# A delta-rule attention with two MoE layers on one core: the second layer's weights converted six tiles later

## The chip, the cores and the metric

The kernel runs on one core of one Trainium2 chip. The metric is the device time of one execution in microseconds (us); three runs of the kernel before gave 930.33, 930.95 and 936.27, and their median is 930.95 us. Lower is better.

## What is computed

A recurrent attention over 768 steps (4 batches, 8 heads of width 48) writes 3072 tokens of width 384. Two dense layers follow on each token: the first goes 384 to 1024 with a softmax-weighted activation and a layer norm and back to 384, the second goes 384 to 2048, takes the square of the ReLU, and goes back to 384. Cut to what matters:

```
for t in range(S):                       # attention, k_n = k / |k|
    y[t] = q[t] @ state
    state = state + b[t] * outer(k_n[t], v[t] - k_n[t] @ state)
h = x @ w_in;  s = h * softmax(h)        # first layer
x1 = layer_norm(s) * g_ln @ w_out
r = relu(x1 @ w2_in)                     # second layer
out = (r * r) @ w2_out
```

The weights arrive as 64-bit floats and are needed as 32-bit floats.

## The kernel before, in words

**Tiles.** The tokens are taken as 24 tiles of 128 (`NT`). For every tile TensorE forms the Gram products of keys and queries (`e_tile`, up to ten tiles ahead), a small triangular matrix is inverted for groups of 2 to 4 tiles (`inversion`), the blocks of the inverse are loaded back from DRAM in two shapes and joined (`prep`), a product with them is formed for each half of the tile (`zstep`), and two recurrent steps follow (`chain`). The groups start at tiles 0, 4, 7, 11, 15, 19 and 22 (`G0`). The first group is inverted on VectorE, the other six on GpSimd, by hundreds of small multiply and add instructions (lines 900 and 917) that end in line 942. ScalarE then makes the transposed copy (line 959), and both forms go to DRAM (`tscr`, `uscr`), from where `prep` loads them (`tbd`, `t`).

**First layer.** It runs beside the attention, two to four tiles behind it: `moe1_front` (transposes on line 1207, products into `p_h` on line 1218, softmax and norm sums on ScalarE and VectorE), `moe1_back` (transposes on line 1320, the high and low parts `zh` and `zl` from `split`, line 433) and `moe1_out` (products into `p_x` on line 1340, for two tiles at once). Each float product is done as three products of rounded parts, hence `hi` and `lo` in `split`.

**Second layer.** It starts when the attention is over, since its weights take the SBUF space of the attention pool (`open_m2`). From about 545 us to the end TensorE runs only its products (lines 1483 and 1527).

**Weights.** `load_w` turns a chunk of 64-bit numbers into 32-bit ones: a DMA into one of two `raw` buffers, one ScalarE instruction (line 466) into one of two `wst` buffers, and four VectorE instructions (lines 474, 485, 500, 510). The chunks of the second layer, 12 of `w2_in` and 16 of `w2_out`, are then written back to DRAM as 32-bit numbers (`load_w2`, `w2s` and `wos`), because there is no room for them in SBUF yet; `fill_w2` reads them again when the pool of the second layer is open.

**What sets the order.** Every instruction group is handed to `Plan.add` with its engine, an estimated cost, what it reads and writes, a priority, and further operations that it must come after (`after`). `Plan.order` then simulates the engines with these costs, forwards and backwards in 12 rounds: the first round goes by the priorities given, each later one by how late an operation may be as the round before found it, and the best round's order is emitted. The order on every engine, on SyncE's DMA queue too, is thus fixed before the kernel runs; an instruction that is late holds up all that stand behind it on its engine. A priority counts in the first round only; an operation in `after` counts in all.

The change touches the loop over tiles (line 1616), where the second layer's chunks are handed to the planner, and the first VectorE instruction of `load_w` (line 474).

Of the kernel before, what the change touches and what calls it, by code (L numbers as in the profile page):

```python
# [114 lines left out]
class Plan:  # L115
# [19 lines left out]
    def add(self, eng, cost, fn, r=(), w=(), prio=0.0, size=0, after=()):  # L135

        i = len(self.ops)
        deps = set(after)
        for k in r:
            if k in self.writer:  # L140
                deps.add(self.writer[k])
            if k in self.BANKS:

                deps.update(j for j in self.readers.get(k, ()) if self.ops[j][0] != eng)
            self.readers.setdefault(k, []).append(i)
        for k in w:
            if k in self.writer:
                deps.add(self.writer[k])
            deps.update(self.readers.get(k, ()))
            self.writer[k], self.readers[k] = i, []  # L150
        deps.discard(i)
        self.ops.append((eng, cost, fn, prio, deps, size))
        return i
# [108 lines left out]
def c_dve(n, fast=False):  # L262
    return 0.07 + n / (1920.0 if fast else 960.0)


def c_act(n, sbuf=False):
    return (0.095 if sbuf else 0.053) + n / 1200.0
# [8 lines left out]
def tile_delta_moe_moe(  # L276
# [16 lines left out]
    plan = Plan()  # L293
# [4 lines left out]
    def dma(dst, src, r=(), w=(), prio=0.0, size=0):  # L298

        return add("sp", 0.06, lambda: nc.sync.dma_start(dst(), src()), r, w, prio, size, gate)  # L300
# [40 lines left out]
    def const(i, n, u=False):  # L341
        return (cst_u if u else cst)[:, i : i + 1].to_broadcast([P, n])
# [96 lines left out]
        )  # L439


    n_w, first_inv = [0], []

    def load_w(src, n, prio):

        i = n_w[0] % 2
        n_w[0] += 1
        w = wst_[i][:, 0:n]
        kw, kr = ("A", "wst", i), ("A", "raw", i)
        if src.dtype == F32:  # L450
            dma(lambda: w, lambda: src, (), [kw], prio - 1, P * n * 4)
            return w, kw
        raw, wu = raw_[i][:, 0:n], w.bitcast(U32)
        up, low = raw[:, :, 1], raw[:, :, 0]
        dma(
            lambda: raw.rearrange("p n t -> p (n t)"),
            lambda: src.bitcast(U32),
            (),
            [kr],
            prio - 1,  # L460
            P * n * 8,
        )
        add(
            "act",
            c_act(n, True),
            lambda: act.activation(out=w, in_=up.bitcast(F32), func=AF.Abs),
            [kr],
            [kw],
            prio,
        )  # L470
        add(
            "dve",
            c_dve(n),
            lambda: v.scalar_tensor_tensor(
                out=w, in0=w, scalar=F64_LO, in1=const(3, n), op0=ALU.max, op1=ALU.min
            ),
            [],
            [kw],
            prio,
            after=first_inv,  # L480
        )
        add(
            "dve",
            c_dve(n),
            lambda: v.scalar_tensor_tensor(
                out=wu,
                in0=wu,
                scalar=3,
                in1=const(5, n, True),
                op0=ALU.logical_shift_left,  # L490
                op1=ALU.bitwise_and,
            ),
            [],
            [kw],
            prio,
        )
        add(
            "dve",
            c_dve(n),
            lambda: v.scalar_tensor_tensor(  # L500
                out=wu, in0=up, scalar=0xC0000000, in1=wu, op0=ALU.bitwise_and, op1=ALU.bitwise_or
            ),
            [kr],
            [kw],
            prio,
        )
        add(
            "dve",
            c_dve(n),
            lambda: v.scalar_tensor_tensor(  # L510
                out=wu,
                in0=low,
                scalar=29,
                in1=wu,
                op0=ALU.logical_shift_right,
                op1=ALU.bitwise_or,
            ),
            [kr],
            [kw],
            prio,  # L520
        )
        return w, kw
# [40 lines left out]
    def load_w2(i, prio):  # L563

        if i < 12:
            c, s = i // 4, slice((i % 4) * 512, (i % 4) * 512 + 512)
            w, kw = load_w(w2i[c, :, s], 512, prio)
            dma(lambda: w2s[c][:, s], lambda: w, [kw], [("w2s", c, i % 4)], prio, P * 2048)
        else:
            f = i - 12  # L570
            w, kw = load_w(w2o[f], DM, prio)
            dma(lambda: wos[f], lambda: w, [kw], [("wos", f)], prio, P * DM * 4)
# [193 lines left out]
    def gammas(g, prio):  # L766

        n = 2 * (G0[g + 1] - G0[g])
        w = n * NP
        be, gm = be_[g % 2], gm_[g % 2]  # L770
        x, y, u = nrm_[g % 3].rearrange("p s q -> p (s q)")[:, 0:w], ny[:, 0:w], ntt[:, 0:w]
        b = be[:, 0:w]
        kn = [("A", "nrm", g % 3, s) for s in range(n)]
        kbe, ky, kgm = ("A", "be", g % 2), ("A", "ny"), ("A", "gm", g % 2)
        if n < GS:
            add("pool", 0.1, lambda: pool.memset(be[:, w:], 0.0), (), [kbe], prio - 1)
        dma(
            lambda: b,
            lambda: betat[:, 2 * G0[g] * NP : 2 * G0[g + 1] * NP],
            (),  # L780
            [kbe],
            prio - 1,
            P * 128,
        )

        def dv(fn, r, w):
            add("dve", c_dve(HB), fn, r, w, prio)

        dv(
            lambda: v.tensor_tensor(out=x, in0=x, in1=const(0, w), op=ALU.max), (), kn  # L790
        )
        rsqrt(y, x, u, HB, kn, [ky], prio)
        dv(lambda: v.tensor_tensor(out=x, in0=x, in1=y, op=ALU.mult), [ky], kn)
        dv(
            lambda: v.tensor_tensor(out=x, in0=x, in1=const(2, w), op=ALU.add), (), kn
        )
        dv(lambda: v.reciprocal(y, x), kn, [ky])
        dv(lambda: v.tensor_tensor(out=b, in0=b, in1=y, op=ALU.mult), [ky], [kbe])
        dv(lambda: v.tensor_tensor(out=b, in0=b, in1=y, op=ALU.mult), [ky], [kbe])

        gt = p_z[:, NP * 112 : NP * 112 + HB]

        def mm():
            for hb in range(4):
                sl = slice(hb * HB, hb * HB + HB)
                pe.matmul(gt[sl], be[sl], ident[sl, sl], start=True, stop=True)

        add("pe", 0.22, mm, [kbe], [("A", "z")], prio)
        add("act", c_act(HB), lambda: act.copy(gm, gt), [("A", "z")], [kgm], prio)
# [779 lines left out]
    for t in range(NT + 3):  # L1589
        if t < NT:  # L1590
            for g in range(2, NG):
                if t == max(1, G0[g] - 5):
                    gammas(g, t + PR["inv"])
                    inversion(g, "pool", t + PR["inv"])
            tp = t + PR["first"] if t < T1 else t
            chain(2 * t, tp + PR["chain"])
            zstep(2 * t + 1, tp + PR["z"])
            chain(2 * t + 1, tp + PR["half"] + PR["chain"])
            if t + 1 < NT:
                tp = t + PR["first"] if t + 1 < T1 else t  # L1600
                prep(t + 1, tp + PR["prep"])
                zstep(2 * t + 2, tp + PR["z1"] + PR["z"])
            if t + LA < NT:
                e_tile(t + LA, t + PR["e"])
                norms(t + LA, t + PR["norms"])
        if t == NT - 1:
            add("x", 0.0, open_m2, (), [*plan.keys("A"), ("m2",)], t)
        if 2 <= t < NT + 2:
            moe1_front(t - 2, t + PR["mf"])
            if t == NT + 1:  # L1610
                add("x", 0.0, open_mb, [("m2",)], [*plan.keys("W"), ("mb",)], t)
        if t >= 3:
            moe1_back(t - 3, t + PR["mb"])
            if (t - 3) % 2:
                moe1_out((t - 3) // 2, t + PR["mo"])
        for i in (2 * t - 4, 2 * t - 3):
            if 0 <= i < 28:
                load_w2(i, t + PR["w2"])
    add("x", 0.0, open_ps, [("m2",)], [("h", 0), ("h", 1), ("tr",), ("x1",), ("ps",)], NT + 3)
    for n in range(4):  # L1620
# [75 lines left out]
```

## Time and profile before

| | us |
|---|---|
| median of the three runs | 930.95 |
| the profiled execution | 934.67 |
| its span, first to last instruction | 932.7 |
| TensorE busy (matmul) | 864.9 |
| VectorE busy | 519.5 |
| ScalarE busy | 487.3 |
| GpSimd busy | 365.2 |

The profile shows one execution on the chip. PE is TensorE's matmuls, PEld its weight loads, DVE is VectorE, ACT is ScalarE, POOL is GpSimd, and SP or SPq is SyncE, which issues all DMAs. PEclk is the share of full speed that TensorE's clock was granted: 1.00 is 2.4 GHz and 0.50 is 1.2 GHz. "A <- B" in a table of waits means that A stood idle until B was done. L433 is line 433 of the kernel.

### The profile page before, as it was taken

How to read it: one execution, taken by the hardware profiler on the slowest of the kernel's cores; microseconds unless marked ns; L12 is line 12 of the kernel's file. 1: busy time of each engine (PE TensorE's matmuls, PEld its weight loads, DVE VectorE, ACT ScalarE, POOL GpSimd, SP SyncE). 2: the span in 40 equal slices, each digit the busy share in tenths (PEclk: the TensorE clock that was granted, in tenths of full speed). 3: DMA queues.
4: the chain of work that ended last, by engine and by line, in shares of the span. 5: the costliest groups of instructions: out<-in, count | busy, mean ns of one | idle time of the engine just before them, and what ended most of it. 6: DMA issues, size and time to landing. Idle time of an engine off the chain costs nothing.

```text
span 932.7 us, 23189 instructions
## 1 busy us (share of the span) xinstructions
PE 864.9 (93%) x9144; PEld 806.9 (87%) x9144; DVE 519.5 (56%) x1063; ACT 487.3 (52%) x1069; POOL 365.2 (39%) x898
## 2 busy tenths in 40 slices
PE   7349789989998999999998999999999999999998
PEld 6347678867887888888887999999999999999998
DVE  6996887786856896634435655343343434343332
ACT  5335787666756766666565644333333434343333
POOL 6399889899747947987500000000000000000000
PEclk8566898989998999999999999999999999999999
DMA  8827876858687577442314432001010101000000
GB/s 243 212 85 192 202 225 177 231 169 235 201 221 198 144 226 184 120 143 68 101 44 136 132 106 63 15 6 47 1 51 1 51 1 52 1 26 1 26 1 26
DMA packets 129244, 101.75 MB, mean 109 GB/s; under 512 B 84080, under 2 KB 106608, under 8 KB 129136
## 3 DMA queue, kind: packets, MB, share of 16 engines
q1 hardware_dynamic: 129136, 100.28, 38.4%
q8 instruction: 72, 1.18, 0.6%
q14 instruction: 36, 0.29, 0.1%
HBM read 70.88 MB, written 29.36 MB: 107 GB/s over the span
## 4 chain that ended last, share of the span: by engine, by line
PE 70%; DVE 8%; POOL 8%; DMA 7%; SPq 2%; ACT 2%; issue 2%; POOLq 0%; ACTq 0%; DVEq 0%
PE acc L1527 22%; PE h L1483 21%; PE p_x L1340 8%; PE p_h L1218 7%; PE p_z L1098 3%; POOL it L917 2%; POOL itmp L900 2%; SPq L300 2%; PE p_tr L1320 2%; PE p_a L1139 2%; DVE itmp L900 1%; DVE it L917 1%; DMA vt<-in_vtok_dram 1%; PE p_ep L684 1%; DMA m<-in_ktok_dram 1%
## 5 line engine op out<-in xcount | busy, mean ns | idle before, releaser
L1504 DVE TENSOR_TENSOR xt<-xt 128x384 f32<-128x384 f32 x128 | 71.5, 559 | 163.7 <-ACT xt L1496 163.5
L1496 ACT ACTIVATE xt<-h 128x384 f32<-128x384 f32 x128 | 62.9, 492 | 167.8 <-PE h L1483 167.7
L1483 PE MATMUL h<-x1h,w2h 128*128 128x384 f32 x384 | 128.9, 336 | 0.0
L1483 PE MATMUL h<-x1l,w2h 128*128 128x384 f32 x384 | 128.6, 335 | 0.0
L1483 PE MATMUL h<-x1h,w2l 128*128 128x384 f32 x384 | 128.3, 334 | 0.0
L917 POOL TENSOR_TENSOR it<-it,itmp 128x72 f32<-128x72 f32 (+37 forms) x255 | 110.1, 446 | 5.1
L900 POOL TENSOR_TENSOR itmp<-it 128x72 f32<-128x72 f32 (+37 forms) x255 | 109.3, 443 | 1.9
L1527 PE MATMUL acc<-woh,xl 128*128 128x384 f32 x258 | 87.4, 339 | 0.0
L1527 PE MATMUL acc<-wol,xh 128*128 128x384 f32 x258 | 87.3, 338 | 0.0
L1340 PE MATMUL p_x<-zh,wgh 128*128 128x256 f32 x288 | 85.7, 298 | 1.5 <-ACT xo L1354 1.5
L1527 PE MATMUL acc<-woh,xh 128*128 128x384 f32 x258 | 86.9, 337 | 0.0
L1340 PE MATMUL p_x<-zl,wgh 128*128 128x256 f32 x288 | 81.5, 283 | 1.0 <-DVE zl L433 1.0
L1340 PE MATMUL p_x<-zh,wgl 128*128 128x256 f32 x288 | 81.6, 283 | 0.0
L433 DVE TENSOR_TENSOR xl<-xt,xh 128x384 fp32r<-128x384 f32 x86 | 48.0, 558 | 45.7 <-ACT xh L428 45.5
L1483 PEld LDWEIGHTS h<-x1h,w2l 128*128 128x128 f32 x384 | 72.1, 188 | 0.0
L1483 PEld LDWEIGHTS h<-x1h,w2h 128*128 128x128 f32 x384 | 72.1, 188 | 0.0
L1483 PEld LDWEIGHTS h<-x1l,w2h 128*128 128x128 f32 x384 | 72.1, 188 | 0.0
L428 ACT CAST xh<-xt 128x384 fp32r<-128x384 f32 x86 | 44.1, 513 | 47.8 <-DVE xt L1504 46.7
L1218 PE MATMUL p_h<-w1h,xh 128*128 128x512 f32 x144 | 65.0, 451 | 0.1
L1098 PE MATMUL p_z<-m,tbd 128*128 128x112 f32 x384 | 59.9, 305 | 0.7 <-ACT tbd L1068 0.5
L1218 PE MATMUL p_h<-w1h,xl 128*128 128x512 f32 x144 | 59.1, 410 | 0.1
L1218 PE MATMUL p_h<-w1l,xh 128*128 128x512 f32 x144 | 58.8, 408 | 0.0
(197 smaller groups left out, 2152.0 us busy)
## 6 DMA issues: line engine op xcount, KB each, us to landing
kql<-in_kin_dram SPq DMA_DIRECT2D x24, 512.0 KB
kqe<-in_kine_dram SPq DMA_DIRECT2D x40, 192.0 KB
raw<-in_w2i_dram SPq DMA_DIRECT2D x12, 512.0 KB
raw<-in_w2o_dram SPq DMA_DIRECT2D x16, 384.0 KB
gscr<-g SPq DMA_DIRECT2D x21, 256.0 KB
m<-in_ktok_dram SPq DMA_DIRECT2D x24, 192.0 KB
vt<-in_vtok_dram SPq DMA_DIRECT2D x24, 192.0 KB
x1scr<-xo SPq DMA_DIRECT2D x12, 384.0 KB
```

The source lines that it names most:

```text
L300: return add("sp", 0.06, lambda: nc.sync.dma_start(dst(), src()), r, w, prio, size, gate)
L428: add("act", c_act(n), lambda: act.copy(hi(), src()), r, [w[0]], prio)
L433: lambda: le.tensor_tensor(out=lo(), in0=src(), in1=hi().bitcast(F32), op=ALU.subtract),
L900: lambda tm=tm, j=j, nr=nr, w_=w_, c0=c0, c1=c1: eng.tensor_tensor(out=tm, in0=it[:, j + 1 :, j : j + 1].to_broadcast([P, nr, w_]), in1=it ...
L917: lambda tm=tm, j=j, c0=c0, c1=c1: eng.tensor_tensor(out=it[:, j + 1 :, c0:c1], in0=it[:, j + 1 :, c0:c1], in1=tm, op=ALU.add,),
L1098: pe.matmul(zp[:, p].rearrange("q (j c) -> q j c", j=7), tb[:, i * NP + p], m[:, i, :, p], start=True, stop=True,)
L1218: pe.matmul(p_h[:, sl], xx[:, c], ww[:, c, sl], start=(c == 0 and k == 0), stop=(c == 2 and k == 2),)
L1340: pe.matmul(p_x1[:, 0 : 2 * P], ww[:, f, c * P : c * P + P], zz[:, f], start=(f == 0 and k == 0), stop=(f == 7 and k == 2),)
L1483: pe.matmul(late["h2", ih], late[ww][:, c, s], xx[:, c], start=(c == 0 and k == 0), stop=(c == 2 and k == 2),)
L1496: lambda: act.activation(out=rt, in_=late["h2", ih], func=AF.Relu),
L1504: lambda: v.tensor_tensor(out=gg, in0=rt, in1=rt, op=ALU.mult),
L1527: pe.matmul(late["acc", a], gg[:, a * P : a * P + P], late[ww][:, f], start=(f == 0 and k == 0), stop=(f == 15 and k == 2),)
```

## The change

The chunks of the second layer are handed out in the loop pass of tile 8 and the following ones, no longer from tile 2 on, and the first VectorE instruction of each chunk must come after the `zs` copy of the second half of that pass's tile. So the two chunks of pass t wait for `zstep(2t+1)`. The DMA of the raw chunk and the ScalarE instruction have no such condition. The instructions themselves are the same, 28 chunks with four VectorE instructions each.

```diff
-    n_w, first_inv = [0], []
+    n_w, first_inv, w2_gate = [0], [], []
...
-            after=first_inv,
+            after=[*first_inv, *w2_gate],
...
-        for i in (2 * t - 4, 2 * t - 3):
+
+        for i in (2 * t - 16, 2 * t - 15):
             if 0 <= i < 28:
+                w2_gate[:] = [plan.writer["A", "zs", 1]]
                 load_w2(i, t + PR["w2"])
```

The planner works the whole order out anew. VectorE in the kernel before, between the recurrent steps of tiles 6 and 7 (`wst` are the weights under conversion, `zl` the low part for the first layer, `m` the masked Gram product, `sc` a softmax maximum):

```order
L718 TENSOR_TENSOR m_177<-p_ep,mask 128x256
L433 TENSOR_TENSOR zl<-p_tr,zh 128x4x128
L474 SCALAR_TENSOR_TENSOR wst_223<-wst_223,cst 128x512
L485 SCALAR_TENSOR_TENSOR wst_223<-wst_223,cst 128x512
L500 SCALAR_TENSOR_TENSOR wst_223<-raw_221,wst_223 128x512
L510 SCALAR_TENSOR_TENSOR wst_223<-raw_221,wst_223 128x512
L433 TENSOR_TENSOR zl<-p_tr,zh 128x4x128
L1233 TENSOR_REDUCE sc_162<-p_h 128x1
```

Here a whole chunk stands between two `zl`. The corresponding place on VectorE in the changed kernel, just ahead of the second step of tile 6:

```order
L718 TENSOR_TENSOR m_177<-p_ep,mask 128x256
L433 TENSOR_TENSOR zl<-p_tr,zh 128x4x128
L755 TENSOR_REDUCE nrm_192<-sq_189 128x4
L755 TENSOR_REDUCE nrm_192<-sq_190 128x4
L433 TENSOR_TENSOR zl<-p_tr,zh 128x4x128
L1233 TENSOR_REDUCE sc_162<-p_h 128x1
```

The conversion is gone from between them; on VectorE the first chunk of the second layer now stands behind the first recurrent step of tile 8. SyncE's queue in the kernel before, where the inverse of the third group (tiles 7 to 10) is written and read back (`tscr`, `uscr` the two forms in DRAM; `tbd`, `t_0`, `t_1` the blocks for `prep`):

```order
L300 DMA w2s_108<-wst_224 128x512
L300 DMA raw_222<-in_w2i_dram 128x1024
L300 DMA tscr_84<-it_212 128x1024
L300 DMA uscr_91<-ia 128x1024
L300 DMA w2s_109<-wst_223 128x512
L300 DMA raw_221<-in_w2i_dram 128x1024
L300 DMA tbd_199<-tscr_84 32x8x32 x4
L300 DMA tbd_198<-tscr_84 32x8x32 x2
L300 DMA t_1_201<-uscr_91 32x4x32 x4
```

Two DMAs of weights stand between the write of the inverse and its reads. The same place in the changed kernel:

```order
L300 DMA vt_196<-in_vtok_dram 128x384
L300 DMA tscr_84<-it_212 128x1024
L300 DMA uscr_91<-ia 128x1024
L300 DMA tbd_199<-tscr_84 32x8x32 x4
L300 DMA tbd_198<-tscr_84 32x8x32 x2
L300 DMA t_1_201<-uscr_91 32x4x32 x4
```

They have moved behind, and the reads follow the writes at once. VectorE in the kernel before at the first recurrent step of tile 22 (`r` opens a step, `fac` are norm factors of the first layer):

```order
L433 TENSOR_TENSOR xl_161<-p_tr,xh_159 128x384
L1251 SCALAR_TENSOR_TENSOR ez_164,sc_162<-ez_164,p_h 128x1024
L1171 TENSOR_TENSOR r_207<-vt_196,p_a 128x192
L1289 SCALAR_TENSOR_TENSOR sm_all<-sm_all,cst 128x3
L1296 SCALAR_TENSOR_TENSOR fac<-sm_all 128x3
L1303 SCALAR_TENSOR_TENSOR fac<-s_all,fac 128x3
```

There is no weight here; the last chunk of the kernel before stands at tile 17. The same step on VectorE in the changed kernel:

```order
L474 SCALAR_TENSOR_TENSOR wst_223<-wst_223,cst 128x384
L1171 TENSOR_TENSOR r_207<-vt_196,p_a 128x192
L485 SCALAR_TENSOR_TENSOR wst_223<-wst_223,cst 128x384
L474 SCALAR_TENSOR_TENSOR wst_224<-wst_224,cst 128x384
L500 SCALAR_TENSOR_TENSOR wst_223<-raw_221,wst_223 128x384
L433 TENSOR_TENSOR zl<-p_tr,zh 128x4x128
L510 SCALAR_TENSOR_TENSOR wst_223<-raw_221,wst_223 128x384
L485 SCALAR_TENSOR_TENSOR wst_224<-wst_224,cst 128x384
```

The last two chunks now stand among the steps of tile 22, and the pool of the second layer opens only behind them.

## Rows read from the trace of the kernel before

**Rows 1.** Stages: length, busy PE PEld DVE ACT POOL (instructions), PEclk, DMA share, GB/s.
```profile
160.00:245.00 85.00, 77.59 (x1103) 68.21 (x1102) 63.41 (x112) 57.65 (x132) 80.89 (x208) 0.95 0.72 208
245.00:300.00 55.00, 50.70 (x830) 43.01 (x831) 36.86 (x78) 34.93 (x86) 28.36 (x70) 0.94 0.78 214
300.00:390.00 90.00, 86.26 (x1408) 74.47 (x1409) 71.64 (x143) 58.22 (x136) 69.62 (x182) 1.00 0.67 182
390.00:480.00 90.00, 89.11 (x1459) 77.76 (x1459) 34.86 (x84) 54.35 (x117) 57.37 (x183) 1.00 0.33 93
480.00:520.00 40.00, 37.35 (x474) 33.72 (x461) 19.25 (x32) 25.10 (x52) 0.00 (x0) 0.96 0.32 93
```

**Rows 2.** TensorE's waits from 160 to 245 us: total, times, longest.
```profile
PE p_tr L1207 <- DVE zl L433: 3.4, 1, 3.4
PE p_ep L684 <- ACT tbd L1068: 1.7, 2, 1.4
PE p_x L1340 <- DVE zl L433: 1.0, 1, 1.0
PE p_tr L1320 <- DVE zl L433: 0.8, 1, 0.8
```

**Rows 3.** TensorE alone around 205 us: length, busy, granted clock, DMA share, GB/s.
```profile
202.00:205.00 3.00, 0.00 (x0) 0.65 1.02 255
205.00:207.00 2.00, 1.97 (x36) 0.50 0.20 31
...
209.00:211.00 2.00, 1.74 (x37) 0.82 0.32 54
```

**Rows 4.** VectorE's costliest groups, 160 to 245 us: busy, mean ns | idle before.
```profile
L510 DVE SCALAR_TENSOR_TENSOR wst<-raw,wst 128x512 uint32<-128x512 uint32 x11 | 10.5, 952 | 0.2
L474 DVE SCALAR_TENSOR_TENSOR wst<-wst,cst 128x512 f32<-128x512 f32 x11 | 9.2, 841 | 7.1 <-ACT wst L466 7.1
L485 DVE SCALAR_TENSOR_TENSOR wst<-wst,cst 128x512 uint32<-128x512 uint32 x11 | 8.4, 763 | 0.2
L500 DVE SCALAR_TENSOR_TENSOR wst<-raw,wst 128x512 uint32<-128x512 uint32 x11 | 7.7, 703 | 0.2
```

**Rows 5.** VectorE in order of time: start, length, instruction.
```profile
182.05 1.30 DVE L474 SCALAR_TENSOR_TENSOR wst<-wst,cst 128x512 f32<-128x512 f32 x1 [1.72 <-ACT wst L466]
...
185.57 0.68 DVE L433 TENSOR_TENSOR zl<-p_tr,zh 128x512 fp32r<-128x512 f32 x1
...
202.11 0.86 DVE L485 SCALAR_TENSOR_TENSOR wst<-wst,cst 128x512 uint32<-128x512 uint32 x1
...
204.29 0.68 DVE L433 TENSOR_TENSOR zl<-p_tr,zh 128x512 fp32r<-128x512 f32 x1
```

**Rows 6.** Lines 917 (first pair) and 900, two stretches: length, DVE, POOL busy.
```profile
160.00:197.00 37.00, 0.00 (x0) 12.26 (x30) 0.97 0.75 218
395.00:452.00 57.00, 0.00 (x0) 21.16 (x61) 1.00 0.32 87
...
160.00:197.00 37.00, 0.00 (x0) 13.39 (x30) 0.97 0.75 218
395.00:452.00 57.00, 0.00 (x0) 19.93 (x59) 1.00 0.32 87
```

**Rows 7.** SyncE's queue in order of time: start, length of the issue.
```profile
199.19 0.33 SPq L300 DMA_DIRECT2D uscr<-ia  x1
199.62 0.37 SPq L300 DMA_DIRECT2D w2s<-wst  x1
200.09 0.73 SPq L300 DMA_DIRECT2D raw<-in_w2i_dram  x1
...
461.91 0.33 SPq L300 DMA_DIRECT2D uscr<-ia  x1
```

**Rows 8.** ScalarE in order of time, the zs copies around the third group.
```profile
177.03 0.52 ACT L1109 COPY zs<-p_z 128x448 f32<-128x448 f32 x1
...
213.09 0.52 ACT L1109 COPY zs<-p_z 128x448 f32<-128x448 f32 x1
```

## The prediction

> **What bounds the kernel now.** I read the table of busy time by stage first, then TensorE's waits in the stages where it idles, then what VectorE, GpSimd and the DMA queue did at those waits. In the stage table [rows 1] the reader is to see that TensorE is the bound nearly everywhere from 160 us on, and how it is not: in 160 to 245 us it is busy 77.6 of 85 us at a mean granted clock of 0.95, in 245 to 300 us 50.7 of 55 at 0.94, in 300 to 390 us 86.3 of 90 at 1.00, and in 390 to 480 us 89.1 of 90 at 1.00. What the change can win is therefore idle time and slow clock, not work: TensorE's instructions are the same. A second at half speed costs half a second, so a mean clock c over a stretch costs its length times (1 - c). That gives for 160 to 245 us 7.4 us idle and 85 x 0.05 = 4.3 us of clock; for 245 to 300 us 4.3 and 3.3 us; for 300 to 390 us 3.7 and nothing; for 390 to 480 us 0.9 and nothing; for 480 to 520 us 2.7 and 1.6. After that TensorE runs without a gap to the end, and nothing of the change reaches there. VectorE is the second thing to see in the same rows: 63 of 85 us and 72 of 90 us while weights are converted, 35 of 90 us once they are done.
>
> TensorE's four largest waits between 160 and 245 us [rows 2] are 3.4 us for a `zl` in front of the transposes of line 1207, 1.0 and 0.8 us for two other `zl`, and 1.7 us for ScalarE's `tbd` copies. The fine windows [rows 3] show what followed the 3.4 us wait: TensorE did nothing from 202 to 205 us, its clock fell to 0.50 (1.2 GHz) and was back at full speed within 209 to 211 us. A mean of 0.82 over the last two of these us puts the return at about 209.7 us; from 205 us until then it worked at half speed, which lost some 2.4 us.
>
> **What leaves the stage of tiles 5 to 8.** In 160 to 245 us VectorE ran eleven chunks, four instructions each, for 10.5 + 9.2 + 8.4 + 7.7 = 35.8 us [rows 4]. In the changed kernel none of them can start before the second half of tile 8, and the raw loads behind the first two wait with them for a buffer. What was beside other work costs nothing; what stood in front of TensorE is this. The conversion from 182.05 us and its three followers hold VectorE up to the `zl` of 185.57 us [rows 5], and that is the 1.0 us wait: it goes. A conversion instruction of 0.86 us starts at 202.11 us ahead of the `zl` of 204.29 us, which ends the 3.4 us wait; with the one before it about 1.6 us of that wait is a direct queue.
>
> The rest of that wait has another cause, and it too hangs on the conversions. Tile 7 needs the inverse of the third group. The `zs` copies show a hole from 177.03 to 213.09 us [rows 8] in which the recurrence stood still, and TensorE ran out of first-layer work near its end. The inverse left for DRAM at 199.19 us, with a weight write and a raw load of 0.37 and 0.73 us ahead of the reads [rows 7]. GpSimd was late, since its small instructions are slower while VectorE converts: lines 917 and 900 take 12.26 + 13.39 = 25.7 us for 60 instructions in 160 to 197 us, against 21.16 + 19.93 = 41.1 us for 120 of the same kinds in 395 to 452 us, where no weight is converted [rows 6]. At the second rate 60 would take 20.5 us; the mix of sizes differs somewhat, so about 5 us of delay is an estimate. With the 1.1 us of the queue tile 7 can start some 6 us sooner. That covers the 1.8 us left of the 3.4 us wait, and the 0.8 us wait, whose `zl` sat behind the copy of the inverse on ScalarE. The `tbd` waits stay: they are ScalarE's own work.
>
> The Trainium skill (SBUF — State Buffer, section "SBUF: two separate sides") says why: VectorE and GpSimd share one pair of ports under "an exclusive lock, not a bandwidth split", and a VectorE instruction with two SBUF inputs contends with GpSimd ones that read SBUF. The trace agrees, with 25.7 us against 20.5 [rows 6]. The rule speaks against the change as much as for it, because conversions moved to later tiles block the inversions there; what that would give is the second rival below.
>
> So the stage loses 1.0 + 3.4 + 0.8 = 5.2 us of idle time and 2.4 us of slow clock, 7.6 us together. Its bounds: nothing, if the idle time only turns up at another wait, and 7.4 + 4.3 - 0.9 = 10.8 us, if the stage comes to run like 390 to 480 us.
>
> **What arrives later.** The chunks come at the same pace as before, 28 over tiles 8 to 22 in place of 5 to 17, so 245 to 390 us keeps about its load and I give it no term. Bounds: it could lose its 7.6 us of idle time and clock as the order is drawn anew, or gain as much. In 390 to 480 us there were no conversions; now VectorE gets some thirteen chunks there. The nearest row is 300 to 390 us, with VectorE at 71.6 us: TensorE idled 3.7 us there against 0.9 [rows 1]. That makes +2.8 us; bounds 0 and, with one slow-clock stretch like that of 205 us more, 5.2.
>
> **The end of the attention.** The last two chunks stand among tile 22's steps, and their write to DRAM lies ahead of the opening of the second layer's pool. VectorE has room there (34.9 of 90 us busy [rows 1]) and SyncE's queue waits for the chain anyway. The last inverse leaves at 461.91 us [rows 7]; slowed like the third group's it leaves about 5 us later. What hides that is the first layer's work, which keeps TensorE 89.1 of 90 us busy before 480 us [rows 1]. I take 0; if that cover is gone it costs the 5 us and more, below.
>
> **Sum.** -7.6 + 2.8 = -4.8 us. The trace is of an execution of 934.67 us (span 932.7 and 2.0 around it), which makes 929.9. That execution lies 3.7 us above the median of the runs shown, 930.95, and the same sum from the median gives 926.2 us. This is the forecast. A measurement of this kernel can tell about 1% (9.3 us) from no change.
>
> **Rivals.** *More than the named waits.* If VectorE was behind in the whole stretch from 160 to 300 us, and with it free TensorE runs there as in 390 to 480 us, then 7.4 + 4.3 + 4.3 + 3.3 = 19.3 us shrink to 0.9 x 140 / 90 = 1.4, and with the +2.8 the sum is -15.1: 916 us. For it speaks that both slow-clock stretches lie here. Against it, the stage from 245 us keeps its conversions, and no `tbd` wait is VectorE's.
>
> *The lock moves along.* If the inversion of tiles 22 and 23 sets the end of the attention, what is saved at tile 7 is waited out there. Then there is no gain; the inverse is 5 us late, a wait of that size brings a slow-clock stretch of 2.4 us, and the crowded VectorE costs its 2.8: +10.2, which is 941 us. It decides from the point at which TensorE's other work runs out before tile 22's blocks arrive. For it speaks that after 480 us TensorE idles 2.7 us with the clock at 0.96, so the end is tight; against it, GpSimd was idle for 33 of 90 us from 390 to 480 us and for 27 of 55 from 245 us, room to catch up [rows 1].
>
> *Nothing moves.* The planner draws a new order, one wait goes and another comes, or the gate shifts the VectorE instructions without TensorE feeling it: 931 us. For it speaks that the waits are few and single, and that two of the four were ScalarE's; against it, that 35.8 us leave the busiest stretch of VectorE.
>
> **Chances.** The forecast has 0.43 with a range of its own from 922 to 930 us; the large gain 0.28; nothing 0.18; the later lock 0.11. The range from 915 to 936 us takes in the large gain and the new order's scatter and leaves out most of the 941 us case. Faster by over 1% (under 921.6 us) is the large gain and a tail of the forecast, 0.32; slower by over 1% (over 940.3 us) is the later lock with little beside it, 0.10; the rest is 0.58.
>
> **What would show it.** Right: in the changed profile no conversion on VectorE between about 160 and 235 us, GpSimd's lines 917 and 900 at some 0.34 us each before the third inverse, that inverse at DRAM near 193 us instead of 199, no wait over 2 us for `zl` and no clock under 1.00 around tile 7; from 390 to 480 us VectorE near 70 us busy and TensorE idle for 3 to 4 us. Wrong: a wait of several us in front of tile 22's `prep` products or at the opening of the second layer, new slow-clock stretches between 390 and 520 us, or idle time before 160 us that differs by more than 3 us, since the sum takes that part as unchanged.

## The result and the profile after

The changed kernel takes 923.57 us (median of 9 runs, 917.67 to 927.88), the kernel before in the same comparison 931.75 us (9 runs, 930.33 to 936.32). The ratio is 0.9898 with an interval from 0.9873 to 0.9923: 1.0% faster. The forecast was 926.2 us, a gain of 4.8 us; measured were 8.2 us between the medians. The profiled execution took 926.2 us with a span of 924.3 us, 8.4 us under the span of before.

The stages of the changed kernel, with the columns of [rows 1] and the two stages ahead of them:

```profile
0.00:80.00 80.00, 45.59 (x433) 43.11 (x436) 64.16 (x205) 33.89 (x89) 54.70 (x105) 0.67 0.66 173
80.00:160.00 80.00, 69.04 (x1088) 57.80 (x1087) 61.63 (x120) 62.58 (x148) 71.44 (x157) 0.87 0.77 207
160.00:245.00 85.00, 82.39 (x1342) 73.15 (x1342) 43.20 (x91) 60.36 (x145) 69.93 (x216) 0.98 0.53 145
245.00:300.00 55.00, 52.34 (x766) 45.07 (x759) 42.70 (x89) 37.04 (x86) 35.15 (x76) 0.94 0.79 233
300.00:390.00 90.00, 86.96 (x1501) 76.63 (x1500) 67.49 (x128) 58.30 (x136) 76.08 (x198) 0.98 0.62 176
390.00:480.00 90.00, 86.98 (x1355) 75.10 (x1356) 55.55 (x117) 55.83 (x118) 52.42 (x150) 0.96 0.47 144
480.00:520.00 40.00, 38.99 (x379) 35.71 (x378) 23.98 (x42) 26.95 (x53) 0.00 (x0) 1.00 0.42 129
```

Read as in the prediction, idle time plus length times (1 - clock), these rows and the same rows of other kernels give TensorE's loss by stage in us. "Narrowed" is the load taken off VectorE with the order kept (experiments 1 and 2 below); "repeated" is a second profiled execution of the changed kernel (experiment 9). Each column is one execution.

| stage, us | before | before's order, narrowed | after | after repeated | after's order, narrowed | forecast of the change | found |
|---|---|---|---|---|---|---|---|
| 0 to 160 | 85.2 | 81.6 | 82.2 | 82.1 | 85.0 | 0 | -3.0 |
| 160 to 245 | 11.7 | 9.6 | 4.3 | 4.0 | 6.7 | -7.6 | -7.4 |
| 245 to 300 | 7.6 | 5.3 | 6.0 | 5.1 | 3.9 | 0 | -1.6 |
| 300 to 390 | 3.7 | 0.7 | 4.8 | 2.2 | 1.7 | 0 | +1.1 |
| 390 to 480 | 0.9 | 0.9 | 6.6 | 10.3 | 4.5 | +2.8 | +5.7 |
| 480 to 520 | 4.2 | 4.2 | 1.0 | 1.0 | 1.0 | 0 | -3.2 |

The last column is after minus before and adds up to the 8.4 us of the spans. Executions of one order differ too. From 0 to 160 us, where the experiments' edits change nothing, four executions of before's order lost 81.6 to 85.2 us and four of the changed one 75.6 to 85.0 (experiments 1, 2, 3, 9, 10 and 11 among them). That is as wide as the whole gain, and the -3.0 can't be told from it. From 160 us on the two executions of the changed kernel agree within 4 us a stage, and within 0.3 us where the gain was forecast; differences of 2 or 3 us between single executions carry little weight.

TensorE's waits from 160 to 245 us, to be set beside [rows 2]: total, times, longest.

```profile
PE p_tr L1207 <- DVE zl L433: 1.1, 1, 1.1
PE p_a L1139 <- DVE s L1182: 1.0, 1, 1.0
PE p_h L1218 <- DVE ez L1251: 0.5, 1, 0.5
```

The 3.4 us wait is 1.1 us now, and the `tbd` wait of 1.7 us, which the sum had left in place, is gone as well. The third group's inverse on SyncE's queue, beside [rows 7]: start, length of the issue.

```profile
193.88 0.33 SPq L300 DMA_DIRECT2D uscr<-ia  x1
194.30 3.28 SPq L300 DMA_DIRECT2D tbd<-tscr  x6
```

It leaves 5.3 us sooner, and its reads stand right behind it. The `zs` copies around it, beside [rows 8]:

```profile
175.47 0.53 ACT L1109 COPY zs<-p_z 128x448 f32<-128x448 f32 x1
...
208.23 0.51 ACT L1109 COPY zs<-p_z 128x448 f32<-128x448 f32 x1
```

Tile 7 starts at 208.23 us, 4.9 us sooner. GpSimd's lines 917 (first pair) and 900 in the two stretches of [rows 6]:

```profile
160.00:197.00 37.00, 0.00 (x0) 13.12 (x37) 1.00 0.57 158
395.00:452.00 57.00, 0.00 (x0) 20.47 (x50) 1.00 0.50 150
...
160.00:197.00 37.00, 0.00 (x0) 12.27 (x36) 1.00 0.57 158
395.00:452.00 57.00, 0.00 (x0) 19.85 (x50) 1.00 0.50 150
```

The mean of one of these instructions was 25.7 / 60 = 0.43 us in the early stretch and 41.1 / 120 = 0.34 in the late one. It is 25.4 / 73 = 0.35 and 40.3 / 100 = 0.40 now: the slowing went where the conversions went. The sizes in the two stretches differ, but single sizes show it too: line 900 on 128x120 took 862 ns in the early stretch and takes 406 now, and on 128x117 in the late one 405 and now 603. VectorE's first conversion of the second layer starts at 230.65 us. Two more stretches of TensorE alone, around tile 7 (as in [rows 3]), and one from the late stage with all engines, as in [rows 1]:

```profile
198.00:202.00 4.00, 2.94 (x41) 0.82 0.29 47
202.00:204.00 2.00, 2.00 (x8) 0.50 0.29 46
```

```profile
440.00:460.00 20.00, 18.05 (x272) 15.60 (x271) 14.50 (x44) 11.85 (x22) 7.15 (x17) 0.83 0.68 216
```

At tile 7 a slow stretch is left, shorter than the one of before; and in the late stage, where the clock had been 1.00 throughout, there is a new one.

### The profile page after: what moved, and what is told of

It is laid out like the page before. It is cut to its first block, busy times and chain, and to the rows that moved or that the text cites. A ratio compares the mean times of both kernels' runs of the same rounds, so it can differ in the third digit from the quotient of the medians.

```text
span 924.3 us, 23182 instructions
## 1 busy us (share of the span) xinstructions
PE 862.9 (93%) x9144; PEld 806.9 (87%) x9144; DVE 515.9 (56%) x1063; ACT 487.0 (53%) x1069; POOL 359.7 (39%) x898
## 4 chain that ended last, share of the span: by engine, by line
PE 75%; DVE 8%; DMA 6%; ACT 4%; POOL 3%; issue 2%; SPq 2%; ACTq 0%; DVEq 0%
PE acc L1527 22%; PE h L1483 22%; PE p_h L1218 9%; PE p_x L1340 9%; PE p_z L1098 3%; DMA kqe<-in_kine_dram 2%; PE p_tr L1320 2%; PE p_ep L684 2%; DVE itmp L900 2%; SPq L300 2%; DVE it L917 1%; PE p_a L1139 1%; PE p_o L1155 1%; POOL itmp L900 1%; POOL it L917 1%
## 5 line engine op out<-in xcount | busy, mean ns | idle before, releaser
L900 POOL TENSOR_TENSOR itmp<-it 128x72 f32<-128x72 f32 (+37 forms) x255 | 107.4, 436 | 2.2
```

Of the source, the lines that this page charges most:

```text
L900: lambda tm=tm, j=j, nr=nr, w_=w_, c0=c0, c1=c1: eng.tensor_tensor(out=tm, in0=it[:, j + 1 :, j : j + 1].to_broadcast([P, nr, w_]), in1=it ...
```

## Experiments

The forecast says that the load of the conversions, on VectorE and through it on GpSimd, was what TensorE waited for. The rival theory: the planner drew a new order, and TensorE's own work falls better in it whatever VectorE carries.

**1. The load out, the order kept: kernel before.** The four VectorE instructions of a second-layer chunk work on one column; the cut shows the first of the four and one of the two callers. The planner's costs stay, so every engine's order is that of before.

```diff
-    def load_w(src, n, prio):
+    def load_w(src, n, prio, live=True):
...
+        k = n if live else 1
...
-                out=w, in0=w, scalar=F64_LO, in1=const(3, n), op0=ALU.max, op1=ALU.min
+                out=w[:, 0:k], in0=w[:, 0:k], scalar=F64_LO, in1=const(3, k), op0=ALU.max, op1=ALU.min
...
-            w, kw = load_w(w2i[c, :, s], 512, prio)
+            w, kw = load_w(w2i[c, :, s], 512, prio, False)
```

> The kernel before with its order on every engine kept, but the four VectorE instructions of each of the second layer's 28 chunks work on one column in place of 512 or 384; the second layer's weights are therefore not converted. Theory (load: the conversions cost time where they stand, through VectorE's queue and GpSimd's slowing): nearly all idle time and slow clock of 160 to 390 us above the floor of 390 to 480 us goes, so 12 to 18 us less than before, 914 to 920 us. Rival (luck of the order: the gain came because the planner drew another order): 928 to 932 us.

Measured: 924.73 us (4 runs, 921.62 to 927.72), ratio 0.9862 (0.9815 to 0.9909): neither the theory's 914 to 920 us nor the rival's 928 to 932. The load taken out is thus worth some 1.4% of the kernel before, 0.9 to 1.9% by the interval. It is not all of the load: on one column an instruction still took 0.25 to 0.37 us in the mean, and the 28 chunks 34.8 us of VectorE in place of some 85. But the stage of tiles 5 to 8 is not where this shows. Its row, and TensorE's waits in it (one line was added to the kernel, so L1208 is 1207 of before):

```profile
160.00:245.00 85.00, 78.80 (x1138) 69.47 (x1137) 44.94 (x117) 59.57 (x137) 65.66 (x217) 0.96 0.73 211
```

```profile
PE p_tr L1208 <- DVE zl L433: 2.3, 1, 2.3
PE p_ep L1051 <- ACT ys L1058: 1.4, 1, 1.4
PE p_ep L685 <- ACT tbd L1069: 1.0, 1, 1.0
PE p_x L1341 <- DVE zl L433: 0.8, 1, 0.8
```

VectorE is down from 63.4 to 44.9 us, the inverse leaves at 194.54 us, tile 7 starts at 208.57 us, all as in the changed kernel; and TensorE still loses 9.6 of the 11.7 us. What VectorE did at the wait of 2.3 us, start and length:

```profile
199.24 1.21 DVE L1252 SCALAR_TENSOR_TENSOR ez<-ez,p_h 128x1024 f32<-128x1024 f32 x1
...
200.38 0.69 DVE L433 TENSOR_TENSOR zl<-p_tr,zh 128x512 fp32r<-128x512 f32 x1
...
201.12 0.55 PE L1208 MATMUL p_tr<-ident,xt 128*128 128x128 f32 x3 [2.27 <-DVE zl L433]
```

The first layer's own pass over `ez`, 1.21 us, stands ahead of the `zl`. In the changed kernel the planner put the two the other way round:

```profile
197.86 0.68 DVE L433 TENSOR_TENSOR zl<-p_tr,zh 128x512 fp32r<-128x512 f32 x1
198.62 1.22 DVE L1251 SCALAR_TENSOR_TENSOR ez<-ez,p_h 128x1024 f32<-128x1024 f32 x1
```

Of the 3.4 us some 1.1 went with the load. Of the 2.3 left, 1.2 more are gone in the changed kernel, where two instructions that have nothing to do with weights are exchanged. That the exchange alone does it is read from the two traces and was not tried. The same pass stood ahead of the `zl` of 204.29 us in the kernel before, between the two rows that [rows 5] shows there:

```profile
203.15 1.21 DVE L1251 SCALAR_TENSOR_TENSOR ez<-ez,p_h 128x1024 f32<-128x1024 f32 x1
```

**2. The same in the changed kernel's order.** The same edit, in the changed kernel.

> The changed kernel with its order kept and the same instructions narrowed to one column; the second layer's weights are not converted. Theory (load): it comes to within 4 us of the same edit on the kernel before, some 5 to 10 us under the changed kernel, 914 to 919 us, since what remains of the two orders is alike once the load is out. Rival (luck of the order): it keeps the lead of 8 us over the same edit on the kernel before, about 921 us.

Measured: 920.08 us (4 runs, 917.14 to 922.56), ratio 0.9802 (0.9752 to 0.9852); 4.65 us under experiment 1 on the same chip. That is nearer to the rival's 921 us than to the theory's 914 to 919. With the load out of both, the new order is 0.5% better by the medians of four runs each; the two ranges overlap. The load costs 1.4% in the old order and, by 0.9802 against 0.9898, about 1.0% in the new one. By these figures the change's 1.0% is the sum of two parts: some 0.6% from the order and some 0.4% from the load standing where it hurts less. Each of the two ratios is known to 0.5% either way, so that the split itself is an estimate and neither part is shown by it alone.

**3. Only the chunks of the early stretch narrowed, kernel before.**

```diff
-            w, kw = load_w(w2i[c, :, s], 512, prio)
+            w, kw = load_w(w2i[c, :, s], 512, prio, i >= 11)
```

> The kernel before with its order kept, and only the first eleven chunks of the second layer, those of 160 to 245 us, narrowed to one column (these eleven are not converted). Theory (load): the 7 us that the changed kernel gained in that stretch come without any new order, 922 to 926 us. Rival (luck of the order): 929 to 932 us.

Measured: 931.26 us (10 runs, 923.08 to 937.73), ratio 0.9941 (0.9900 to 0.9981). The time is the rival's (929 to 932 us); the theory's 922 to 926 is missed. The stage, in a profiled execution that was the fastest of the ten:

```profile
160.00:245.00 85.00, 78.62 (x1178) 69.44 (x1177) 45.93 (x119) 60.84 (x142) 65.12 (x215) 0.98 0.76 216
```

The loss is 6.4 + 1.7 = 8.1 us, 3.6 less than before. Freeing exactly this stretch of VectorE gives half of the 7.4 us that the changed kernel won in it, in this one execution.

**4. The shift without the wait.** The chunks are handed out six tiles later, but nothing holds them; they go to nearly the same tiles as before, in an order drawn anew. The edit is against the changed kernel.

```diff
             if 0 <= i < 28:
-                w2_gate[:] = [plan.writer["A", "zs", 1]]
                 load_w2(i, t + PR["w2"])
```

> The shift of six loop passes alone, without the added condition, so that only the priorities of the planner's first round change. The conversions stay at tiles 5 to 17 in the order, while the rest of the order is drawn anew. Theory (load): 928 to 934 us, as before. Rival (luck of the order): it may land anywhere from 920 to 940 us, the gain of 8 us included.

Measured: 931.9 us (7 runs, 927.24 to 934.53), ratio 0.9942 (0.9909 to 0.9976). The new row and the old load:

```profile
160.00:245.00 85.00, 79.18 (x1153) 69.42 (x1145) 64.10 (x116) 60.12 (x137) 81.21 (x209) 0.96 0.72 209
```

VectorE and GpSimd are as loaded as before (64.1 and 81.2 us), and the kernel is 0.6% faster than the kernel before (0.2 to 0.9% by the interval). A new order alone does that; both expectations allowed for it.

**5 to 8. Controls: orders drawn anew, conversions where they were.** A priority that counts only in the planner's first round is moved by one or four tiles, in the kernel before (5 and 6) and in the changed one (7 and 8).

```diff
-    "w2": 2.92,
+    "w2": 1.92,
```

> The kernel before with only the planner's first-round priority of the conversions moved by one (1.92 for 2.92): another order is drawn, the conversions stay at tiles 6 to 17. Theory (the place of the conversions decides, whatever the draw): ratio to the kernel before 0.994 to 1.003, like e4_shift_no_gate's 0.994. Rival (luck of the draw): anywhere from 0.985 to 1.01, so that the draws without the gate reach the changed kernel's 0.990 about as often as not.

> The same with a priority of -1.08: a third order without the gate. Theory (place): ratio 0.994 to 1.003. Rival (luck): anywhere from 0.985 to 1.01.

> The changed kernel with a first-round priority of 1.92 for the conversions: another order with the gate, conversions at tiles 9 to 22. Theory (place): ratio to the kernel before 0.984 to 0.993, as the changed kernel's 0.990. Rival (luck): its lead is lost in a new draw, 0.992 to 1.005.

> The same with a priority of -1.08: a third order with the gate. Theory (place): ratio 0.984 to 0.993. Rival (luck): 0.992 to 1.005.

The second value is -1.08. Measured, ten runs each, against one kernel before on one chip:

| experiment | median us | ratio | interval | loss 160 to 245 us |
|---|---|---|---|---|
| 5, before, 1.92 | 928.17 | 0.9960 | 0.9940 to 0.9980 | 7.6 |
| 6, before, -1.08 | 932.04 | 0.9999 | 0.9966 to 1.0033 | 8.4 |
| 7, after, 1.92 | 929.50 | 0.9947 | 0.9910 to 0.9983 | 9.6 |
| 8, after, -1.08 | 926.54 | 0.9933 | 0.9900 to 0.9967 | 4.0 |

Experiments 5 and 6 lie where the theory of the place had them; 7 and 8 just miss its 0.984 to 0.993 and lie in the rival's range.

Orders without the wait on `zs` (before, 4, 5, 6) stand at 1.000, 0.994, 0.996 and 1.000, mean 0.9975; orders with it (after, 7, 8) at 0.990, 0.995 and 0.993, mean 0.9926. The later place of the conversions is worth about 0.5% by these means, 4.6 us, and the draw of an order scatters by some 0.3% either way. With four and three draws the 0.5% is not settled more closely. In the stage itself the losses overlap: before's place gives 7.6 to 11.7 us, the later place 4.0 to 9.6. The late stage of 7, then of 8:

```profile
390.00:480.00 90.00, 88.21 (x1466) 75.96 (x1452) 55.59 (x121) 56.29 (x124) 62.96 (x172) 1.00 0.50 150
390.00:480.00 90.00, 89.12 (x1477) 77.17 (x1475) 56.26 (x122) 56.70 (x125) 49.09 (x129) 1.00 0.46 139
```

With VectorE as busy there as in the changed kernel (55.6 and 56.3 us), these orders lose 1.8 and 0.9 us, against 0.9 in the kernel before.

**9. The changed kernel again, and 10, its late chunks narrowed** (chunks 17 to 27, by `i < 17` in the place of experiment 3's condition).

> The changed kernel once more, as the measure for the other three runs on this chip: ratio 0.987 to 0.993 if its first figure of 0.990 holds; 0.993 to 0.997 if that first figure was a good day and its draw is no better than the two other draws with the gate (0.9947, 0.9933).

> The changed kernel with its order kept and its last eleven chunks, those of tiles 17 to 22, narrowed to one column (these eleven are not converted). It prices their new place without a new draw. Theory (the prediction's sum): the new place costs 2.8 us, so 3 us under the changed kernel. The two traces as read since (390 to 480 us loses 6.6 us in place of 0.9) say 5 to 6 us under. Rival (the late place is free, since TensorE has other work): within 1.5 us of the changed kernel.

Measured: 924.22 us (4 runs, 919.22 to 926.53), ratio 0.9867 (0.9798 to 0.9937), and 921.31 us (4 runs, 917.81 to 924.24), ratio 0.9853 (0.9796 to 0.9909). The first lies just below 0.987 to 0.993, the range in which the first figure was to hold. The medians lie 2.9 us apart, as the forecast term of 2.8 would have it, but the intervals overlap widely: the time doesn't settle this term. The late stage of 9, then of 10:

```profile
390.00:480.00 90.00, 83.35 (x1286) 71.32 (x1285) 51.78 (x111) 51.93 (x110) 53.50 (x166) 0.96 0.45 130
```

```profile
390.00:480.00 90.00, 87.27 (x1455) 75.44 (x1453) 39.30 (x116) 56.35 (x120) 41.08 (x135) 0.98 0.43 127
```

With the load out the stage still loses 2.7 + 1.8 = 4.5 us, as in experiment 2, against 0.9 in before's order. Between 440 and 460 us TensorE is busy for 17.97 to 18.05 of 20 us in all of them, narrowed or not, with the clock between 0.83 and 0.92: some 3.6 us of the late price belong to this order, and the load adds 2 to 6 us on top, by single executions. In the orders of experiments 7 and 8, with the load in place, there is next to no price: in those two executions the late place did not cost TensorE this time.

**11. The lock by itself, kernel before.** VectorE's queue stays filled, but the 28 chunks' four instructions each become one that takes a single operand from SBUF. The cut shows the first of the four.

```diff
-            lambda: v.scalar_tensor_tensor(
+            lambda: v.tensor_reduce(
+                out=w[:, 0:4],
+                in_=raw.bitcast(F32)[:, :, 1].rearrange("p (k j) -> p k j", k=4),
+                axis=AX.X,
+                op=ALU.add,
+            )
+            if not live
+            else v.scalar_tensor_tensor(
                 out=w, in0=w, scalar=F64_LO, in1=const(3, n), op0=ALU.max, op1=ALU.min
```

> The kernel before with its order kept; the four VectorE instructions of each of the second layer's chunks are replaced by sums over the same 512 or 384 columns that read one SBUF operand, some 0.55 to 0.7 us each (the second layer's weights are not converted). VectorE's queue stays as full, the two-operand reads go. Theory (the lock on the shared ports carries a good part): GpSimd's lines 917 and 900 fall back to about 0.34 us each in 160 to 197 us, the third inverse leaves some 5 us sooner, and the time is 0.988 to 0.995 of before, a third or more of the way to e1_before_none's 0.986. Rival (only VectorE's queue matters): 0.996 to 1.002, whether or not GpSimd gets faster.

Measured: 930.92 us (10 runs, 927.64 to 934.76), ratio 0.9957 (0.9922 to 0.9993), between the theory's range (up to 0.995) and the rival's (from 0.996). The first instruction of a chunk, with its shortest, median and longest duration in ns, in the kernel before (all 42 chunks) and then here (the 28 replaced):

```profile
L474 DVE SCALAR_TENSOR_TENSOR wst<-wst,cst x42: 545/711/2094, 63.1 to 384.5; 128x384 f32<-128x384 f32 x24, 128x512 f32<-128x512 f32 x18
```

```profile
L474 DVE TENSOR_REDUCE wst<-raw x28: 540/554/687, 165.8 to 378.7; 128x4 f32<-128x384 f32 x16, 128x4 f32<-128x512 f32 x12
```

The one-operand instruction took 687 ns at most, the two-operand one up to 2094. GpSimd is faster beside it. Lines 917 and 900 of before, L945 and L928 here, from 160 to 197 us:

```profile
160.00:197.00 37.00, 0.00 (x0) 11.53 (x34) 0.97 0.79 225
...
160.00:197.00 37.00, 0.00 (x0) 10.52 (x34) 0.97 0.79 225
```

That is 22.05 / 68 = 0.32 us each in place of 0.43. The replaced instructions also write four results a partition and not 384 or 512, so the second operand was not changed by itself. The inverse leaves at 196.14 us, 3.1 us sooner (5 were expected). At the wait in front of line 1207 (1235 here) VectorE and TensorE stood like this:

```profile
199.12 0.68 DVE L474 TENSOR_REDUCE wst<-raw 128x4 f32<-128x512 f32 x1
199.83 0.69 DVE L492 TENSOR_REDUCE wst<-raw 128x4 f32<-128x512 f32 x1
...
202.70 0.66 PE L1235 MATMUL p_tr<-ident,xt 128*128 128x128 f32 x3 [2.27 <-DVE zl L433]
```

Two weight instructions of 1.4 us together still stand ahead of the `ez` pass and the `zl`, and the wait is 2.3 us, just as in experiment 1, where they took 0.6. So the 1.1 us that left this wait need not have been a queue of conversions.

The gain is 0.4%, less than a third of experiment 1, and again not in the stage of tiles 5 to 8, where this execution lost 7.4 + 5.9 = 13.4 us; it idled 0.5 us from 300 to 390 us, where the kernel before idled 3.7. Part of the 0.4% may be the shorter load: the 28 chunks take 67.6 us of VectorE here, in the kernel before some 85.

**12. A version that might beat both: a cheaper conversion in the changed kernel.** Both bounds of the clamp as numbers, so the constant tile isn't read.

```diff
-            lambda: v.scalar_tensor_tensor(
-                out=w, in0=w, scalar=F64_LO, in1=const(3, n), op0=ALU.max, op1=ALU.min
+            lambda: v.tensor_scalar(
+                out=w, in0=w, scalar1=F64_LO, scalar2=F64_HI, op0=ALU.max, op1=ALU.min
```

> The changed kernel with its order kept, and the first VectorE instruction of every weight chunk, both layers' 42, written with two immediate scalars and one tensor operand in place of two tensor operands. If it takes half the time, 0.3 to 0.37 us for 0.55 to 0.69, VectorE saves about 12 us of work. Theory (load on VectorE and the lock cost time where they stand): 2 to 5 us under the changed kernel, a version better than both. Rival (this form holds the shared ports too, or the waits end elsewhere): within 1.5 us of it or slower.

Measured: 922.09 us (8 runs, 919.09 to 928.90), ratio 0.9886 (0.9847 to 0.9925), against 0.9867 for experiment 9 on the same chip. By the medians it is 2.1 us under experiment 9, by the ratios it is slower: no gain that can be told. The instruction takes 349 ns at its shortest instead of 546, but up to 3327. That longest one, and GpSimd in the same stretch, start and length:

```profile
413.62 3.33 DVE L474 TENSOR_SCALAR wst<-wst 128x384 f32<-128x384 f32 x1
```

```profile
413.59 0.11 POOL L930 MEMSET idle<- 128x16 f32 x1
413.66 0.78 POOL L900 TENSOR_TENSOR itmp<-it 128x135 f32<-128x135 f32 x2
414.39 0.79 POOL L917 TENSOR_TENSOR it<-it,itmp 128x135 f32<-128x135 f32 x2
...
416.61 0.12 POOL L930 MEMSET idle<- 128x16 f32 x1
416.76 0.43 POOL L900 TENSOR_TENSOR itmp<-it 128x112 f32<-128x112 f32 x1
```

GpSimd's pairs follow each other without a gap, and the VectorE instruction ends at 416.95 us. Its shortest duration of 0.35 us, counted back from there, gives 416.60 us, about where the last pair of that chain ends and only the 0.12 us instruction of line 930 follows. The Trainium skill (SBUF — State Buffer, section "Who interferes with whom") names this operation among those that can take both ports, and adds that who issues first decides; the 3.33 us beside this chain of GpSimd instructions fit that, though no run here shows what held the instruction.

## Why the prediction was right and where it was wrong

**The time.** 926.2 us forecast, 923.57 measured, inside the forecast's own range of 922 to 930 and with the right sign. That the sum came out near the truth is in part luck, since its errors cancel: the early gain has its size, but mostly not for the reason given; the late price was twice as large as forecast; and the end of the attention gave back 3.2 us that the sum had at 0. The stage from 0 to 160 us, outside the sum, differed by another 3.0 us, which can't be told from scatter.

**The step that failed: "the stage loses 1.0 + 3.4 + 0.8 = 5.2 us of idle time and 2.4 us of slow clock" because VectorE's conversions leave it.** Its links up to TensorE are confirmed: GpSimd at 0.35 us an instruction, the inverse at 193.88 us against the forecast 193, the reads directly behind it, tile 7 4.9 us sooner (some 6 forecast), no `zl` wait over 2 us. The last link is not. In experiment 1 everything up to tile 7 is as early, and 9.6 of the 11.7 us stay lost; in experiment 3 it is 8.1. By these single executions the load accounts for 2.1 to 3.6 of the 7.4 us of the stage. The rest, as far as these rows show, came with the order drawn anew; the exchange of `ez` and `zl` is probably among it, which is argued and not shown. Another draw with the later place (experiment 7) lost 9.6 us in this stage, no less than the old order without the load. The prediction had read the 3.4 us wait as a queue of conversions plus a late inverse. It left out the `ez` pass of 1.21 us in the same stretch of VectorE's queue, and took some 1.6 us of the wait for conversions queued ahead, where experiment 11, with that queue still full, has a wait no longer than that of experiment 1. It also left out that a sooner tile only fills TensorE's idle time if TensorE's own order has it there in time.

**"245 to 390 us keeps about its load and I give it no term."** The sum of the two stages changed by only -0.5 us, but it is the place where the load hurts in the old order: experiment 1 gained 2.3 and 3.0 us there.

**"+2.8 us" for 390 to 480 us.** Mis-sized: +5.7 us, and +9.4 in the repeated execution. The idle part was close in one of them (3.0 us against 3 to 4 forecast, 6.7 in the other), but new slow-clock stretches, which the prediction had only in its bounds, cost 3.6 us in either. By experiments 2 and 10 about 3.6 us come with this order even without load. The stage has nine chunks and not some thirteen, and VectorE was busy 55.6 us, not 70. Nor is it a price of the load on VectorE alone: with the same load there, experiments 7 and 8 lost 1.8 and 0.9 us.

**"The end of the attention. I take 0."** -3.2 us, and it is the order's: the loss from 480 to 520 us is 4.2 us in before's order with and without load (2.7 in experiment 3, 6.2 in 11), and 0.9 to 1.0 in five executions of after's order, but 3.6 and 4.6 in the two other draws with the later place (7 and 8).

**The rivals.** *More than the named waits* had TensorE losing 1.4 us from 160 to 300 us; it lost 10.3. *The lock moves along* is half true. GpSimd's instructions from 395 to 452 us did slow from 0.34 to 0.40 us, but the last inverse left at 452.63 us, 9.3 us sooner than in [rows 7], and nothing was waited out at the end. The slowing that this rival needs is there, but GpSimd, busy 52.4 of the 90 us from 390 to 480, had room for it. *Nothing moves* came close for the stage in experiment 1: most of what the named waits gave by themselves turned up at others.

**The signs.** Of the signs named, "no clock under 1.00 around tile 7" failed in the first execution (0.50 from 202 to 204 us); in the repeated one the whole stage from 160 to 245 us had 1.00, so this sign hung on one execution. No conversion was to stand on VectorE until about 235 us, and the first came at 230.65. And one of the signs of being wrong came: a new slow-clock stretch between 390 and 520 us, in both executions.

What stays open: that the change makes this kernel about 1% faster was measured twice, but not how much of it is the later place and how much the draw. By the means of seven orders the place is worth 0.5%, with a scatter of 0.3% from draw to draw. The late price was not measured apart from the order in time, only in the stage's rows.

## What to carry to other kernels

When a planner redraws the order, an edit has two effects, the load it moves and the new draw, and they can be of one size (here some 0.5% each by the means, not settled closely). Price the load alone by shrinking the instructions with the order kept, and price the draw by redrawing the order with a number that doesn't matter, before a gain is credited to a mechanism. A wait that ends with a certain instruction also needs the reading of everything queued ahead of it, not only of what the edit removes.

## What the runs showed of the hardware beside this

A VectorE instruction with one SBUF operand and four results a partition ran beside GpSimd at 540 to 687 ns throughout, while the two-operand ones, 545 ns at their shortest, reached 2094 ns, with GpSimd's instructions a third slower (0.43 against 0.32 us). An instruction that is shorter alone can be held longer: the clamp with two numbers took 349 ns at best in place of 546, and up to 3.33 us beside a chain of GpSimd instructions. And the loss before 160 us came out between 75.6 and 85.0 us in four executions of the same order, as much as this whole change is worth.
